# The last piece of the down weights as twelve loads of 11 or 10 rows, and six filler products in place of ten

## The chip, the cores and the metric

The kernel runs on one core of one Trainium2 chip. The metric is the device time of one execution, in microseconds. The kernel before takes 1277.06 us (median of 3 runs, 1276.95 to 1277.29).

## The reference

One decode step of a transformer layer for 4 sequences, all in bf16. First attention over a cache: 32 heads of 128, 8192 cached positions, so that K and V are 256 MB each. Then a gated feed-forward block of width 1792.

```python
x = A_x                                             # 4 x 1 x 512
q = layernorm(x) @ wq                               # 4 x 32 heads x 128
p = softmax(q @ k_cache^T * 128**-0.5)              # 8192 positions
h = x + (p @ v_cache) @ wo
g, u = layernorm(h) @ w_gate, layernorm(h) @ w_up   # 4 x 1792
h2 = h + (sigmoid(g) * u) @ w_down                  # the output
```

## The kernel before, in words

Each engine has a list of instructions of its own, written out in the order in which it is to run them; semaphores join the lists. A helper `emit` appends an instruction with its waits, and `dma` appends a load and hands back a token, a semaphore with the count that it has when the load has landed. A load of the usual kind adds 16 to it.

All inputs but x are loaded by SyncE (SP), on one DMA queue, in the order of the list at the end of the function: wq (L532), then 32 units of K and 32 of V, each unit 4 heads, 8 MB, 128 rows of 64 KB, one for each partition (L541). They go to three slots of SBUF, and a load waits until its slot has been read. DVE transposes a K unit in 16 chunks (L335), TensorE makes the scores of each chunk (L344), the maximum and the exponentials follow (L361 to L369), and TensorE multiplies with V (L405) and adds the unit's result to a bank of PSUM (L415). After the last V unit SP has 40 nops (L543 and L544). Then it waits until the last K unit has been read (`k_done`) and issues wo (L546), the gate weights (L548) and the up weights (L552). Then it waits for `v_done`, a unit of V, and issues the down weights in three pieces (L555 to L558): tiles 0 to 7, 8 to 11, and 12 and 13, by the bounds in `WDT` (L149). Each piece is one load of 128 rows, of 8, 4 and 2 KB a row, with a semaphore of its own.

The tail works on 4 rows. The attention's result is masked and gathered (L454, L461, L466), multiplied with wo (L475) and added to x (L479, L480). A layernorm follows (L273 to L287), the products with gate and up weights (L492, run once for each), sigmoid (L503), and the product of both on DVE in two halves, each transposed (L509, L512). The down product (L521) has 14 tiles with two matmuls each, one for each half of the columns; a tile waits for its half of the transposes and for its piece of the down weights. It adds to the residual, which TensorE has put in the bank before (L516). At the end DVE and ScalarE copy half of the columns each (L529, L530), ScalarE issues the store (L559), and SP waits for its landing.

`filler(n, turns)` (L386 to L388) puts a loop of products on TensorE whose results nobody reads: `n` products of 512 columns in a turn. It stands at three places: 12 turns of 2 ahead of the last product with V (L452), 5 turns of 2 ahead of the product with wo (L467), 5 turns of 2 ahead of the layernorm's transposes (L481).

```python
WDT = (0, 8, 12, 14)                                                            # L149
filler(2, 5)                                                                    # L467
for i in range(len(WDT) - 1):                                                   # L556
    prog.dma("sp", f"wd{i}", lambda e, i=i: e.dma_start(
        wd_v[:, WDT[i]:WDT[i + 1], :], wd_src[:, WDT[i]:WDT[i + 1], :]), [v_done], tok=t_wd[i])
```

Of the kernel before, what the change touches and what calls it, by code (L numbers as in the profile page):

```python
# [18 lines left out]
class _Prog:  # L19
# [52 lines left out]
    def emit(self, eng, fn, waits=(), incs=1, ch=None):  # L72
        todo = self._waits(eng, waits)
        key = ch or eng
        tok = self.token(key, incs) if incs else None
        self._put(eng, todo, key, fn, incs, 1)
        return tok
# [41 lines left out]
def bass_sequential_preLN__mha_block_cached__glu_gated_glu__decode_kernel(  # L119
# [13 lines left out]
    _, H, S, DH = A_k_cache.shape  # L133
# [15 lines left out]
    WDT = (0, 8, 12, 14)  # L149
# [4 lines left out]
    prog = _Prog({"p2d": "dve", "d2d": "dve", "a2d": "dve", "d2p": "pe", "a2p": "pe",  # L154
                  "d2a": "act", "p2a": "act",
                  "k0": "dve", "k1": "dve", "v2": "pe"})
    emit = prog.emit

    with ExitStack() as es:
# [40 lines left out]
        def reg(slot, off, size):  # L200
            return KV[:, slot * SLOT + off:slot * SLOT + off + size]
# [6 lines left out]
        wd_v = reg(2, 0, NFT * D).rearrange("p (t f) -> p t f", t=NFT)  # L208
# [20 lines left out]
        t_wo = prog.token("wo", 16)  # L229
        t_wg = prog.token("wg", 16)  # L230
        t_wu = [prog.token(f"wu{i}", 16) for i in range(len(WUC) - 1)]
        t_wd = [prog.token(f"wd{i}", 16) for i in range(len(WDT) - 1)]

        t_eps = emit("pool", lambda e: e.memset(eps[:, :], EPS))
        t_x = prog.dma("act", "x", lambda e: e.dma_start(x_bf, A_x.rearrange("b s d -> (b s) d")))
# [36 lines left out]
        def layernorm(src, waits, dst):  # L272
            a = emit("dve", lambda e: e.bn_stats(bst, src), waits)  # L273
            a = emit("dve", lambda e: e.bn_aggr(agg, bst), [a])
            a = emit("act", lambda e: e.activation(std[:, 0:1], agg[:, 1:2], ACT.Sqrt, bias=eps[0:B, :]), [a, t_eps])
            a = emit("dve", lambda e: e.reciprocal(std[:, 1:2], std[:, 0:1]), [a])
            t_row = emit("dve", lambda e: e.tensor_scalar(
                row, src, agg[:, 0:1], std[:, 1:2], op0=ALU.subtract, op1=ALU.mult), [a])

            def f(e):  # L280
                ins = None
                for c in range(NC):
                    ins = e.matmul(cols(bank[XS], c), row[:, c:c + NC * 127 + 1:NC], ident[0:B, 0:B],
                                   start=(c == 0), stop=(c == NC - 1), skip_group_check=True)
                return ins
            a = emit("pe", f, [t_row, t_ident])
            return t_row, emit("dve", lambda e: e.tensor_copy(dst, bank[XS][:, 0:NC * B]), [a])  # L287
# [4 lines left out]
        _, t_xn = layernorm(x_bf, [t_x], xnT)  # L292
# [89 lines left out]
        def filler(n, turns=1):  # L382
            if turns > 1:
                prog.open("pe")
            for _ in range(turns):
                if turns > 1:  # L386
                    prog.begin("pe")
                emit("pe", lambda e: [e.matmul(bank[XS], Lq[:, 0:128], Lq[:, 0:512], start=True, stop=True) for _ in range(n)][-1],  # L388
                     [t_ps0, t_lq[NU - 1]], incs=0)
                if turns > 1:  # L390
                    prog.end("pe")
            if turns > 1:
                prog.close("pe")
# [70 lines left out]
            return ins  # L464
        t_rt = emit("pe", f, [t_oa])
        t_ot = emit("dve", lambda e: e.tensor_copy(OT, bank[QB[0]][:, 0:B * WOJ]), [t_rt])  # L466
        filler(2, 5)  # L467

        emit("act", lambda e: e.activation(dummy[:, 0:1], mask[:, 0:1], ACT.Sqrt), [t_mask])

# [54 lines left out]
        for t in range(NFT):  # L525
            if t == 0:
# [6 lines left out]
                 tok=t_wq)  # L533
        for n, (x, u) in enumerate(order):
            w = t_qp if n == 2 else None
            if n >= 3:
# [3 lines left out]
            src = cache[u // (NU // B), HU * (u % (NU // B)):HU * (u % (NU // B) + 1), :, :].rearrange("h (p r) d -> (h p) (r d)", p=32)  # L540
            prog.dma("sp", f"{x}{slot}", lambda e, src=src, slot=slot: e.dma_start(reg(slot, 0, SLOT), src), [w],  # L541
                     tok=toks[x, u])
        for _ in range(40):  # L543
            emit("sp", lambda e: e.nop(), ch="pad")  # L544
        k_done, v_done = t_kd[NU - 1], t_vd[NU - 2]
        prog.dma("sp", "wo", lambda e: e.dma_start(  # L546
# [7 lines left out]
                     [k_done], tok=t_wu[i])  # L554
        wd_src = B_w_down.rearrange("(p t) f -> p t f", p=128)  # L555
        for i in range(len(WDT) - 1):  # L556
            prog.dma("sp", f"wd{i}", lambda e, i=i: e.dma_start(  # L557
                wd_v[:, WDT[i]:WDT[i + 1], :], wd_src[:, WDT[i]:WDT[i + 1], :]), [v_done], tok=t_wd[i])  # L558
        t_out = prog.dma("act", "out0", lambda e: e.dma_start(out.rearrange("b s d -> (b s) d"), o_sb), t_o)  # L559
        emit("sp", lambda e: e.nop(), [t_out], incs=0)  # L560

# [30 lines left out]
```

## Time and profile before

| what | value |
|---|---|
| median of 3 runs | 1277.06 us |
| the profiled execution's own time | 1276.83 us |
| its span, first to last instruction | 1275.6 us |
| mean granted TensorE clock | 0.815 |
| bytes read from HBM | 550.77 MB |
| mean DMA rate over the span | 432 GB/s |

The profile is of one execution, taken by the hardware profiler. Busy times are per engine: PE is TensorE's matmuls, PEld its weight loads, DVE VectorE, ACT ScalarE, SP SyncE. L521 is line 521 of the kernel; all lines of the code from L232 on shift with the edit, L467 to L468 and L557 to L560, for example. In the timeline a row has the start and the length in microseconds, engine, line, operation, what it writes and reads, and in brackets how long the engine was idle ahead of it and what ended that. In the rows of windows there stand, for each stretch, its length, the busy time of PE, PEld, DVE, ACT and POOL with their instruction counts, the granted clock of TensorE, the mean busy share of the 16 DMA engines, and GB/s. A packet is one row of a load or one completion.

### The profile page before, as it was taken

How to read it: one execution, taken by the hardware profiler on the slowest of the kernel's cores; microseconds unless marked ns; L12 is line 12 of the kernel's file. 1: busy time of each engine (PE TensorE's matmuls, PEld its weight loads, DVE VectorE, ACT ScalarE, POOL GpSimd, SP SyncE). 2: the span in 40 equal slices, each digit the busy share in tenths (PEclk: the TensorE clock that was granted, in tenths of full speed). 3: DMA queues.
4: the chain of work that ended last, by engine and by line, in shares of the span. 5: the costliest groups of instructions: out<-in, count | busy, mean ns of one | idle time of the engine just before them, and what ended most of it. 6: DMA issues, size and time to landing. Idle time of an engine off the chain costs nothing.

```text
span 1275.6 us, 14073 instructions
## 1 busy us (share of the span) xinstructions
PE 779.7 (61%) x4588; PEld 328.5 (26%) x4636; DVE 762.3 (60%) x917; ACT 59.0 (5%) x114; POOL 5.7 (0%) x22
## 2 busy tenths in 40 slices
PE   1676755557755557655567655567555577555577
PEld 0232222223222223222222222222222232222233
DVE  1876665556665557665567655566655566655571
ACT  2000000000000000000000000000000000000001
POOL 1000000000000000000000000000000000000000
PEclk8888877788877788877788777788777888777888
DMA  9999999999999999999999999999999999999998
GB/s 423 432 426 430 427 450 434 430 430 427 454 430 430 430 427 454 432 427 430 430 452 432 427 430 434 450 430 427 430 440 444 430 427 430 442 442 430 430 427 371
DMA packets 10244, 550.83 MB, mean 432 GB/s; under 512 B 1144, under 2 KB 1152, under 8 KB 1408
## 3 DMA queue, kind: packets, MB, share of 16 engines
q1 hardware_dynamic: 10224, 550.77, 99.7%
q8 instruction: 2, 0.03, 0.0%
q10 hardware_dynamic: 16, 0.01, 0.0%
q14 instruction: 2, 0.02, 0.0%
HBM read 550.77 MB, written 0.00 MB: 432 GB/s over the span
## 4 chain that ended last, share of the span: by engine, by line
DMA 60%; PE 20%; DVE 12%; issue 2%; ACT 1%; SPq 0%; DVEq 0%
DMA KV<-in_A_k_cache_dram 58%; PE PS L344 14%; DVE kT L335 12%; PE PS L405 5%; DMA KV<-in_B_w_down_dram 3%; ACT kT L410 1%; PE PS L415 0%; SPq L541 0%; DVE PTz L375 0%; PE PS L521 0%; DVE KV L529 0%; SPq L557 0%; DVEq L112 0%
## 5 line engine op out<-in xcount | busy, mean ns | idle before, releaser
L344 PE MATMUL PS<-kT,Lq 128*128 128x512 bf16 x2048 | 588.7, 420 | 343.5 <-DVE kT L335 326.4
L335 DVE STREAM_TRANSPOSE kT<-KV 128x1024 f32<-128x1024 f32 x512 | 614.4, 1232 | 300.3 <-DMA KV<-in_A_k_cache_dram 237.5
L344 PEld LDWEIGHTS PS<-kT,Lq 128*128 x2048 | 210.3, 103 | 694.6 <-issue 621.7
L375 DVE STREAM_TRANSPOSE PTz<-E_sb 32x512 bf16<-32x512 bf16 x128 | 89.9, 703 | 129.1 <-PE PS L415 125.5
L405 PE MATMUL PS<-KV,PTz 128*16 128x512 bf16 x2048 | 117.0, 381 | 0.0
L379 PE MATMUL PS<-part,headw 128*128 128x2 f32 x64 | 18.8, 363 | 100.4 <-DVE PTz L375 100.4
L369 ACT ACTIVATE E_sb<-PS,negm 128x512 bf16<-128x512 f32 x32 | 22.0, 687 | 1139.4 <-DVE negm L367 1139.4
L405 PEld LDWEIGHTS PS<-KV,PTz 128*16 128x16 bf16 x2048 | 58.9, 111 | 56.3 <-issue 13.6
L415 PE MATMUL PS<-lane,kT 128*128 128x4 f32 x256 | 33.6, 255 | 31.0 <-ACT kT L410 31.0
L362 DVE TENSOR_REDUCE part<-PS 128x1 f32<-128x512 f32 x32 | 22.1, 691 | 38.7 <-PE PS L344 38.7
L415 PEld LDWEIGHTS PS<-lane,kT 128*128 128x128 f32 x256 | 31.0, 191 | 46.2 <-issue 44.8
L379 PEld LDWEIGHTS PS<-part,headw 128*128 128x128 f32 x64 | 16.0, 310 | 103.7 <-DVE PTz L375 103.7
L410 ACT ACTIVATE kT<-PS,rsb 128x512 f32<-128x512 f32 x32 | 22.0, 687 | 61.5 <-PE PS L405 61.5
L388 PE MATMUL PS<-Lq 128*128 128x512 bf16 x27 | 11.0, 462 | 2.9 <-issue 2.5
L328 DVE TENSOR_TENSOR Lq<-q_all,mask 128x32 bf16<-128x32 bf16 x32 | 9.5, 297 | 0.0
L454 DVE TENSOR_TENSOR kT<-PS,mask 128x512 bf16<-128x512 f32 x1 | 0.7, 692 | 13.3 <-PE PS L415 13.3
L367 DVE STREAM_TRANSPOSE negm<-mxr 128x32 f32<-128x32 f32 x32 | 6.8, 212 | 1.1
L364 DVE STREAM_TRANSPOSE turn<-part 128x32 f32<-128x32 f32 x32 | 6.8, 211 | 1.1
L388 PEld LDWEIGHTS PS<-Lq 128*128 128x128 bf16 x44 | 4.8, 116 | 8.3 <-issue 6.1
L322 PEld LDWEIGHTS PS<-Lq,headw 128*128 128x128 bf16 x32 | 3.5, 108 | 12.8 <-issue 11.3
L396 DVE RECIPROCAL rsb<-PS 128x1 f32<-128x1 f32 x32 | 6.3, 197 | 0.7 <-PE PS L379 0.7
L301 PE MATMUL PS<-KV,kT 128*4 128x512 bf16 x32 | 3.6, 627 | 5.0 <-DMA KV<-in_A_wq_dram 5.0
(70 smaller groups left out, 56.7 us busy)
## 6 DMA issues: line engine op xcount, KB each, us to landing
KV<-in_A_wq_dram SPq DMA_DIRECT2D x1, 4096.0 KB, 12.2
KV<-in_A_wo_dram SPq DMA_DIRECT2D x1, 4096.0 KB, 27.2
KV<-in_B_w_gate_dram SPq DMA_DIRECT2D x1, 1792.0 KB, 31.1
KV<-in_B_w_up_dram SPq DMA_DIRECT2D x1, 1792.0 KB, 34.9
KV<-in_B_w_down_dram SPq DMA_DIRECT2D x1, 1024.0 KB, 32.1
KV<-in_A_k_cache_dram SPq DMA_DIRECT2D x32, 49.6
KV<-in_A_v_cache_dram SPq DMA_DIRECT2D x32, 30.7
KV<-in_B_w_down_dram SPq DMA_DIRECT2D x1, 512.0 KB, 32.9
```

The source lines that it names most:

```text
L328: t_lq[u] = emit("dve", lambda e, ix: e.tensor_tensor(dst, bass.AP(raw(q_all), at(ix, 0) * (4 * TU) + 4 * (u - TU * t), [[NU * 4, 128], [1 ...
L335: t_tr[u, c] = emit("dve", lambda e: e.transpose(kT[:, (c % 2) * TW:(c % 2 + 1) * TW], KVw[:, o:o + TW]), w, ch="d2p")
L344: ins = e.matmul(bank[SBK], bass.AP(raw(Lq), ix[-1] * 2 + (128 * t + c % 2), [[528, 128], [1, 128]]), rhs, start=False, stop=False, skip_g ...
L362: a = emit("dve", lambda e: e.tensor_reduce(part[:, 0:1], bank[SBK], AX.X, ALU.max), [t_sc[u, NT - 1], t_pool], ch="d2d")
L364: a = emit("dve", lambda e: e.transpose(turn_[:, :], part[:, :]), [a], ch="d2d")
L369: t_exp[u] = emit("act", lambda e: e.activation(E_sb[:, :], bank[SBK], ACT.Exp, bias=negm[:, 0:1], scale=SCALE, accum_out=part[:, 1:2]), [ ...
L375: return [e.transpose(PTz[32 * q:32 * (q + 1), :].rearrange("p (r q c) -> p r q c", r=4, q=4)[:, :, q, :], E_sb[32 * q:32 * (q + 1), :].re ...
L379: t_sum[u] = emit("pe", lambda e: e.matmul(bank[QB[1]][:, 0:2], headw[:, :], part[:, 0:2], start=True, stop=True), [t_ptz[u], t_selc], ch= ...
L388: emit("pe", lambda e: [e.matmul(bank[XS], Lq[:, 0:128], Lq[:, 0:512], start=True, stop=True) for _ in range(n)][-1], [t_ps0, t_lq[NU - 1] ...
L405: made.append(e.matmul(PS[32 * j:32 * j + 16, ob:ob + 512], lhsT, KV[:, slot * SLOT + 512 * k:slot * SLOT + 512 * (k + 1)], start=(k < 4), ...
L410: t_ocp[u] = emit("act", lambda e: e.activation(O_sb, bank[OBK], ACT.Copy, scale=rsb[:, 0:1]), [t_pv[u], t_rs[u]], ch="a2p")
L415: ins = e.matmul(bass.AP(raw(PS), at(ix, 0) * 4 + (512 * EX + 4 * (u - t)), [[4096, 128], [1, 4]]), O_sb[:, 128 * q:128 * (q + 1)], lane[: ...
```

## The change

The third piece of the down weights, tiles 12 and 13, is no longer one load of 128 rows of 2 KB. It is twelve loads: load `a`, for `a` from 0 to 11, has the rows and partitions a, a + 12, a + 24 and so on, 11 rows for `a` under 8 and 10 rows for the others. All twelve add to the same semaphore, on whose count of 192 the last two tiles wait. The first two pieces are as before. Since SP issues 11 DMAs more, the nops ahead of wo are 29 in place of 40. The filler ahead of the product with wo has 3 turns in place of 5, so six products in place of ten.

```diff
-        t_wd = [prog.token(f"wd{i}", 16) for i in range(len(WDT) - 1)]
+        LAST = [(a, 11 if a < 8 else 10) for a in range(12)]
+        t_wd = [prog.token(f"wd{i}", 16 * (len(LAST) if i == len(WDT) - 2 else 1)) for i in range(len(WDT) - 1)]
...
-        filler(2, 5)
+        filler(2, 3)
...
-        for _ in range(40):
+        for _ in range(29):
             emit("sp", lambda e: e.nop(), ch="pad")
...
-            prog.dma("sp", f"wd{i}", lambda e, i=i: e.dma_start(
-                wd_v[:, WDT[i]:WDT[i + 1], :], wd_src[:, WDT[i]:WDT[i + 1], :]), [v_done], tok=t_wd[i])
+            for a, n in (LAST if i == len(WDT) - 2 else ((0, 0),)):
+                rows = slice(a, a + 12 * (n - 1) + 1, 12) if n else slice(0, 128)
+                prog.dma("sp", f"wd{i}", lambda e, i=i, rows=rows: e.dma_start(
+                    wd_v[rows, WDT[i]:WDT[i + 1], :], wd_src[rows, WDT[i]:WDT[i + 1], :]), [v_done], tok=t_wd[i])
```

## Prediction

> **What bounds the kernel now.** I read the page first (busy shares, the slices, the chain that ended last), then the end of the run: the DMA share in windows, the timeline of the last microseconds, the DMA issues with their times to landing.
>
> ```profile
> PE 779.7 (61%) x4588; PEld 328.5 (26%) x4636; DVE 762.3 (60%) x917; ACT 59.0 (5%) x114; POOL 5.7 (0%) x22
> DMA  9999999999999999999999999999999999999998
> DMA packets 10244, 550.83 MB, mean 432 GB/s; under 512 B 1144, under 2 KB 1152, under 8 KB 1408
> q1 hardware_dynamic: 10224, 550.77, 99.7%
> q10 hardware_dynamic: 16, 0.01, 0.0%
> DMA 60%; PE 20%; DVE 12%; issue 2%; ACT 1%; SPq 0%; DVEq 0%
> ```
>
> No compute engine is over 61% busy, while the sixteen DMA engines (I call each a lane) are busy in every slice. 432 GB/s over 16 lanes is 27 GB/s a lane. Nothing in the change alters the 550 MB, so only the last few microseconds can move. The end of the run in windows (the last two columns are the mean busy share of the 16 lanes, and GB/s):
>
> ```profile
> 1270.50:1271.30 0.80, 0.46 (x4) 0.00 (x0) 0.64 (x2) 0.00 (x0) 0.00 (x0) 1.00 0.97 387
> 1271.30:1271.70 0.40, 0.07 (x2) 0.10 (x4) 0.40 (x2) 0.00 (x0) 0.00 (x0) 1.00 0.56 215
> 1271.70:1273.00 1.30, 1.22 (x22) 0.77 (x23) 0.45 (x2) 0.00 (x0) 0.00 (x0) 1.00 0.16 61
> 1273.00:1273.80 0.80, 0.74 (x12) 0.15 (x6) 0.00 (x0) 0.00 (x0) 0.00 (x0) 1.00 0.00 0
> ```
>
> The share falls from 0.97 to 0.16, which is 2.6 of 16 lanes, and stays there for 1.3 us: most lanes are done by about 1271.5, and two or three run about 1.3 us behind. They don't speed up when the others stop (61 GB/s over 2.6 lanes is 23), so a lane has a limit of its own. The kernel's end hangs on the late lanes:
>
> ```profile
> 1239.43 1.28 SPq L557 DMA_DIRECT2D KV<-in_B_w_down_dram  x3
> 1271.60 0.78 PEld L521 LDWEIGHTS PS<-KV 128*4 128x4 bf16 x16 [1.15 <-DVE KV L512]
> 1272.75 0.31 PEld L521 LDWEIGHTS PS<-KV 128*4 128x4 bf16 x8 [0.37 <-DMA KV<-in_B_w_down_dram]
> 1273.39 0.09 PEld L521 LDWEIGHTS PS<-KV 128*4 128x4 bf16 x4 [0.33 <-DMA KV<-in_B_w_down_dram]
> 1273.85 0.38 ACT L530 ACTIVATE KV<-PS 4x256 bf16<-4x256 f32 x1 [3.50 <-PE PS L521]
> 1274.31 0.27 ACTq L559 DMA_DIRECT2D out_dram<-KV  x1
> KV<-in_B_w_down_dram SPq DMA_DIRECT2D x1, 1024.0 KB, 32.1
> KV<-in_B_w_down_dram SPq DMA_DIRECT2D x1, 512.0 KB, 32.9
> KV<-in_B_w_down_dram SPq DMA_DIRECT2D x1, 256.0 KB, 33.1
> ```
>
> The reader is to see two waits in a row. The four tiles of the middle piece start at 1272.75 after 0.37 us of idling for their DMA, the two of the last piece at 1273.39 after 0.33 us more. Copies follow at 1273.85, the store at 1274.31, the end at 1275.6. The span of 1275.6 belongs to an execution of 1276.83 us (1.23 outside it); the median shown, 1277.06, is 0.23 above that execution. I sum against 1276.83 and add 0.23.
>
> **The change part by part.** *The fillers.* Rows around L467, in which L388 is the filler and L475 the product with wo:
>
> ```profile
> 1259.55 0.63 PE L388 MATMUL PS<-Lq 128*128 128x512 bf16 x1 [0.22 <-issue]
> 1260.41 0.63 PE L388 MATMUL PS<-Lq 128*128 128x512 bf16 x1 [0.22 <-issue]
> 1261.82 2.22 PE L475 MATMUL PS<-KV,kT 128*4 128x512 bf16 x32
> 1268.74 1.69 PE L492 MATMUL PS<-KV,kT 128*4 128x448 bf16 x32 [0.27 <-DVE kT L287]
> 1271.05 0.41 DVE L512 STREAM_TRANSPOSE KV<-KV 128x224 bf16<-128x224 bf16 x1
> 1271.77 0.41 DVE L512 STREAM_TRANSPOSE KV<-KV 128x224 bf16<-128x224 bf16 x1
> 1233.33 0.33 SPq L546 DMA_DIRECT2D KV<-in_A_wo_dram  x1
> KV<-in_A_wo_dram SPq DMA_DIRECT2D x1, 4096.0 KB, 27.2
> 1234.18 0.42 SPq L552 DMA_DIRECT2D KV<-in_B_w_up_dram  x1
> KV<-in_B_w_up_dram SPq DMA_DIRECT2D x1, 1792.0 KB, 34.9
> 1245.40:1248.80 3.40, 2.51 (x5) 1.18 (x8) 0.00 (x0) 0.00 (x0) 0.00 (x0) 0.50 0.78 337
> 1259.10:1262.50 3.40, 2.74 (x12) 1.03 (x18) 0.00 (x0) 0.00 (x0) 0.00 (x0) 0.50 0.97 417
> 1262.50:1265.90 3.40, 2.61 (x31) 0.66 (x24) 0.01 (x1) 0.60 (x1) 0.00 (x0) 1.00 0.99 422
> ```
>
> A turn of two fillers takes 0.86 us at the granted clock of 0.50 (1260.41 less 1259.55); two of five turns go, 1.7 us. wo lands at 1233.33 + 27.2 = 1260.5, so L475 starts at about 1260.6 in place of 1261.82. Until 1262.5 the clock is 0.50: of the 1.2 us won, half is lost again to products run at half clock, so L475 ends 0.6 us earlier, and the layernorm and L492 come 0.6 us earlier (1268.1). The first 16 products of L492 need half of 1.69, to 1268.95; the other 16 need the up weights, which land at 1234.18 + 34.9 = 1269.1. They start at 1269.1 in place of 1269.5: 0.4 us of the 0.6 is left. So the transposes of L512 end at 1271.06 and 1271.78, in place of 1271.46 and 1272.18. There it stops: the first L521 product waits for the first down piece (1239.43 + 32.1 = 1271.5), and the middle piece is later still. **Zero at the end.** If the cover by the DMAs were gone, it would be worth 0.4 us. The clock could undo it: the window 1259.10:1262.50 has 2.74 us of PE work now and about 2.8 to 2.9 after (1.0 of fillers, 1.9 of L475); one with 2.51 at the same clock was followed by full clock. I take no change of clock; another 3.4 us at half clock would delay L475 by up to 0.9 us and the chain after it by at most that much again, most of it in the slack that the down pieces leave: 0 to +0.5.
>
> *SP.* Eleven nops go and eleven DMAs come. Three issues took 1.28 us at L557, so 0.43 each; fourteen end at 1239.43 + 6.0 = 1245.4, 26 us ahead of need, and nothing of SP's is behind them but the last wait. The nops lie before the wait for k_done at L546 (28.6 us of waiting below). Zero.
>
> ```profile
> SPq L546 <- DVE dumm L361: 28.6, 1, 28.6
> GB/s 0 0 0 0 0 0 0 0 0 0 0 0 0 0 0 0 0 0 0 0 0 20 41 21 0 0 0 0 0 0 0 0 0 0 0 0 0 0 0 0
> q10 hardware_dynamic: 8, 0.00, 0.7%
> ```
>
> *The loads.* How many lanes does a load of 11 rows use? The 71 loads of 128 rows on q1 have 9088 rows; 10224 packets less these is 1136 = 71 x 16 completions. The store of four rows (last two rows above, the window 1274 to 1276 in 40 slices of 0.05 us) left 8 packets: four rows, four completions. So a DMA of four rows goes to four lanes with one row and one completion each, and I take 11 and 10 lanes for 11 and 10 rows. In all: ten lanes get 12 rows and 12 completions, one gets 8 and 8, five get none, where each had 8 and one. Packets on q1: 10224 + 128 - 16 = 10336.
>
> From the middle to the last piece the late lanes need 1273.39 - 1272.75 = 0.64 us for 8 rows and a completion; 16 KB at 27 GB/s is 0.60, so a completion costs at most 0.04. Twelve rows and completions cost 0.96 to 1.4 us. The punctual lanes, done at about 1271.5, start the last piece 0.64 before that, at 1270.9, and so end by 1271.9 to 1272.3. If the late lanes are among the five, the last piece no longer ends last.
>
> Next late is then the **middle piece**, which stays on all sixteen lanes and lands for PE at 1272.75 + x, where x is what the new loads do to the late lanes. Four more weight loads, two pairs of products, take 0.31 - 0.09 = 0.22 us, 0.11 a pair. The middle piece's four pairs take 0.44; from the first product of the last piece to the copies it is 1273.85 - 1273.39 = 0.46. The copies start at 1272.75 + x + 0.44 + 0.46 = 1273.65 + x, against 1273.85: **the end moves by x - 0.20.**
>
> x lies between 0 and 0.64. Zero, if a lane's 27 GB/s is a limit of the sender, since the late senders have no more to do than before up to the middle piece. [...] I take the upper end, because the other way in which the late lanes can hurt (below) comes out near it: +0.44.
>
> [...]
>
> **The rivals.**
>
> *Forecast, 0.42:* the writes collide, x is near 0.64. 1276.83 + 0.44 + 0.23 = 1277.50; its own range is 1277.1 to 1277.7, x from 0.24 to 0.84.
>
> *A, the late lanes are relieved, 0.26:* they are among the five, and x is 0. -0.20: 1276.86. For it: the drain at 0.16 is just the work that is taken off them. Against: the last piece is only 0.64 us of a lag of 1.3, and PE is busy 0.44 of those 0.64 anyway.
>
> *B, a late lane is among the eleven, 0.22:* it takes the last piece from 1272.75 on with 12 rows in place of 8: 1273.71 to 1274.15, later by 0.32 to 0.76. 1277.38 to 1277.82. For it: eleven of sixteen lanes are used, and no view says which lanes are late. Against: only 1272.75 stands for all late lanes; one of them may be less late. [...]
>
> *C, slower by more than the bound, 0.05:* a completion holds its lane until its rows are confirmed. Place: the eleven lanes, between rows. The price per completion p makes the last piece 12 x (0.08 + p) long from 1270.9 on; it passes the old landing of 1273.39 from p = 0.13 on and costs over 2.55 us (0.2%) from p = 0.34 on. The store is the nearest row for a whole confirmation: from its packets (1275.05 to 1275.2, slices 22 to 24 above) to the end at 1275.6, p is about 0.4, and the piece would land at 1276.7: +3.3, 1280.4. Against: at most 0.04 between the middle and the last piece, as worked out above.
>
> *D, the loads don't spread, 0.03:* 128 rows on one lane are 128 x 0.08 = 10 us from 1270.9: 1280.9, +7.5, 1284.6. Against: the store's eight packets.
>
> **How the numbers follow.** The forecast with A and B holds 0.90; C, D and the unforeseen 0.10. Predicted: 1277.50. The range goes from A with 0.26 for the scatter of runs and a smaller gain, 1276.6, to the upper end of B with as much, 1278.1. A measurement of this kernel tells about 0.2% (2.55 us) from no change, and the forecast, A and B all lie within that. Slower by over 0.2%: C and D, 0.08. Faster by over 0.2%: 0.01, the half of the unforeseen (no case here is worth 2.5 us). Same: 0.90 and the other 0.01, 0.91.
>
> **What would show it.** Fillers: L475 starts at about 1260.6, the first L521 load still at 1271.6. Loads: 10336 packets on q1, twelve issues at L560 of 0.43 us each. Forecast: the wait before the middle piece's products ends later than 1272.75, at up to 1273.39, and there is no wait before the last four. A: it ends at 1272.75 with no wait behind it, copies at 1273.65. B: the middle piece at 1272.75 and the last four products at 1273.7 or later. C and D: a wait of microseconds before the last four products. Wrong altogether would be a time outside 1276.6 to 1278.1, above all from a change before 1258, where nothing was edited.

## The result, and the profile after

The changed kernel takes 1278.69 us (median of 22 runs, 1277.93 to 1279.42), the kernel before 1276.95 in the same comparison (22 runs, 1276.61 to 1277.39). The ratio is 1.0014, with a 95% interval of 1.0008 to 1.0020: slower by 1.7 us, small but real. The predicted time was 1277.50, with a range up to 1278.1. The profiled execution after took 1278.33 us, 1.50 more than the one before.

The page after, in the rows that answer to those shown of before:

```profile
PE 779.2 (61%) x4586; PEld 327.8 (26%) x4632; DVE 762.4 (60%) x917; ACT 58.9 (5%) x114; POOL 5.7 (0%) x22
DMA  9999999999999999999999999999999999999998
DMA packets 10356, 550.83 MB, mean 431 GB/s; under 512 B 1256, under 2 KB 1264, under 8 KB 1520
q1 hardware_dynamic: 10336, 550.77, 99.6%
```

Bytes and busy times are the old ones, and the packets on q1 are the 10336 that the prediction worked out. The second half of the up products starts at 1269.02, where the prediction had 1269.1 for the landing of their weights in before. So all of it lies in the microseconds behind that. The timeline of after, from the product with wo on:

```profile
1260.54 1.93 PE L476 MATMUL PS<-KV,kT 128*4 128x512 bf16 x32 [0.55 <-DMA KV<-in_A_wo_dram]
1269.02 0.93 PE L493 MATMUL PS<-KV,kT 128*4 128x448 bf16 x16 [0.91 <-DMA KV<-in_B_w_up_dram]
1271.71 0.78 PEld L522 LDWEIGHTS PS<-KV 128*4 128x4 bf16 x16 [1.75 <-DVE KV L513]
1273.42 0.31 PEld L522 LDWEIGHTS PS<-KV 128*4 128x4 bf16 x8 [0.93 <-DMA KV<-in_B_w_down_dram]
1273.42 0.60 PE L522 MATMUL PS<-KV 128*4 128x256 bf16 x8 [0.63 <-DMA KV<-in_B_w_down_dram]
1274.87 0.09 PEld L522 LDWEIGHTS PS<-KV 128*4 128x4 bf16 x4 [1.15 <-DMA KV<-in_B_w_down_dram]
1274.88 0.38 PE L522 MATMUL PS<-KV 128*4 128x256 bf16 x4 [0.86 <-DMA KV<-in_B_w_down_dram]
1275.33 0.37 ACT L531 ACTIVATE KV<-PS 4x256 bf16<-4x256 f32 x1 [6.55 <-PE PS L522]
```

And TensorE's own rows of the down product in before, which the prediction did not show, from the timeline and from the view by line:

```profile
1271.63 2.15 PE L521 MATMUL PS<-KV 128*4 128x256 bf16 x28 [0.68 <-DMA KV<-in_B_w_down_dram]
L521 PE MATMUL PS<-KV x28: 269/272/273, 1271.6 to 1273.5; 128*4 128x256 bf16 x28
```

The reader is to see that before, all 28 products stand in one row of 2.15 us, and that this row hides two waits: each product counts for 0.27 us, while a pair starts 0.11 us behind the last, so a short wait doesn't break the row. The weight loads' rows in the prediction show the waits. The trace also records when each lane's completion reaches its semaphore; I call that a landing. In before the last of the sixteen landings is at 1272.71 for the middle piece and at 1273.35 for the last, and the weight loads follow 0.04 us behind each. After, these landings are at 1273.37 and 1274.83. The waits are longer and break the row in three, with 0.63 us of idling for the middle piece and 0.86 us for the last. From start to start, the middle piece's products come 0.67 later (1273.42 less 1272.75). The last piece could then be used at 1273.42 + 0.44 = 1273.86, and its products start at 1274.87, 1.01 later still. The copies move from 1273.85 to 1275.33, 1.48 of the 1.50 us.

The windows of after, with the DMA share and GB/s in the last two columns:

```profile
1270.50:1271.30 0.80, 0.00 (x0) 0.00 (x0) 0.73 (x4) 0.00 (x0) 0.00 (x0) 1.00 0.94 356
1271.30:1271.70 0.40, 0.00 (x0) 0.00 (x0) 0.40 (x1) 0.00 (x0) 0.00 (x0) 1.00 0.88 262
1271.70:1273.00 1.30, 1.04 (x16) 0.66 (x16) 0.00 (x0) 0.00 (x0) 0.00 (x0) 1.00 0.23 66
1273.00:1273.80 0.80, 0.38 (x8) 0.27 (x8) 0.00 (x0) 0.00 (x0) 0.00 (x0) 1.00 0.02 5
```

From 1271.3 to 1271.7 the lanes are busy for 0.88 (0.56 before) and move 262 GB/s: 0.88 x 16 lanes are 14, so 19 GB/s each, where before had 24 in the same stretch (215 over 0.56 x 16). And after 1273.2 there is no packet at all until the store, as the DMA view of after from 1273.2 to 1276 has it:

```profile
DMA packets 0, 0.00 MB, mean 0 GB/s; under 512 B 0, under 2 KB 0, under 8 KB 0
```

The last packet began at least 1.67 us before the products that wait for it (1274.87 less 1273.2). That time carries no data, only landings: four of the last five, which I take for one lane's, are 0.18 us apart, at 1274.29, 1274.47, 1274.65 and 1274.83 (the fifth is at 1274.34). The packet records show the lane that sent last: its rows start 0.086 us apart, and all twelve rows and completions go out from 1272.14 to 1273.18.

### The profile page after: what moved, and what is told of

It reads as the page before. It is cut to its first block, busy times and chain, and to the rows that moved or that the text cites. A ratio compares the mean times of both kernels' runs of the same rounds, so it can differ in the third digit from the quotient of the medians.

```text
span 1277.1 us, 14063 instructions
## 1 busy us (share of the span) xinstructions
PE 779.2 (61%) x4586; PEld 327.8 (26%) x4632; DVE 762.4 (60%) x917; ACT 58.9 (5%) x114; POOL 5.7 (0%) x22
## 3 DMA queue, kind: packets, MB, share of 16 engines
q1 hardware_dynamic: 10336, 550.77, 99.6%
## 4 chain that ended last, share of the span: by engine, by line
DMA 60%; PE 19%; DVE 13%; issue 2%; SPq 1%; ACT 1%; DVEq 0%
DMA KV<-in_A_k_cache_dram 58%; PE PS L345 14%; DVE kT L336 13%; PE PS L406 5%; DMA KV<-in_B_w_down_dram 2%; ACT kT L411 1%; SPq L560 1%; PE PS L416 0%; SPq L542 0%; DVE PTz L376 0%; PE PS L522 0%; DVE KV L530 0%; DVEq L112 0%
## 5 line engine op out<-in xcount | busy, mean ns | idle before, releaser
L366 DVE TENSOR_SCALAR_CACHE_REDUCE turn<-turn 128x32 f32<-128x32 f32 x32 | 6.0, 187 | 1.1
```

## The experiments

Two terms were to be told apart. For the last piece: it is late because each of its twelve loads costs a lane a time of its own, whatever its size (as in rival C), or because a late lane now has twelve rows in place of eight (rival B). For the middle piece: it is late because rows sent by other lanes go to the partitions that a late lane is still filling (the forecast), or because the new loads get in its way somewhere else. Where a letter stands in an expectation without more, the text below it says what it stood for. The diffs are shortened; in every run the number of nops ahead of wo makes up for the loads added or taken away.

**Each edit alone.** First the fillers:

```diff
-        filler(2, 5)
+        filler(2, 3)
```

> The kernel before with only the filler loop cut from five turns to three. Both theories of the loss (theory L: the loss is all in how the last piece is loaded; rival F: a part of it comes from the fillers, through the clock or the order of the tail) are told apart here. L: within 0.1 us of the kernel before (1276.95), the product with wo starts about 1.2 us earlier, the down products of the first piece at the same time. F: slower by 0.5 us or more.

1276.82 us (11 runs, 1276.56 to 1277.18) against 1276.93; ratio 0.9999, 0.9990 to 1.0008. The timeline:

```profile
1260.62 1.90 PE L475 MATMUL PS<-KV,kT 128*4 128x512 bf16 x32
1271.46 0.77 PEld L521 LDWEIGHTS PS<-KV 128*4 128x4 bf16 x16 [1.55 <-DVE KV L509]
1272.63 0.31 PEld L521 LDWEIGHTS PS<-KV 128*4 128x4 bf16 x8 [0.39 <-DMA KV<-in_B_w_down_dram]
1273.27 0.09 PEld L521 LDWEIGHTS PS<-KV 128*4 128x4 bf16 x4 [0.33 <-DMA KV<-in_B_w_down_dram]
```

The product with wo starts 1.2 us earlier, and the end moves by 0.1: the fillers are worth nothing, as forecast. Then the loads, with the fillers as before:

```diff
-        filler(2, 3)
+        filler(2, 5)
```

> The changed kernel with the five turns of fillers put back, so only the twelve loads (and the 29 nops) are new. L: the whole loss, 1278.4 to 1279.0, with the same two waits before the middle and the last down products. F: clearly nearer to the kernel before, under 1278.0.

1278.93 us (11 runs, 1277.97 to 1279.64); ratio 1.0015, 1.0006 to 1.0025. All of the loss is the loads'. In its timeline the middle piece's products start at 1273.65 and the last piece's at 1274.58, so both waits are there, shared out otherwise than in after.

**Probes behind the old last piece.** Before, with five small loads at the end of the queue and a memset on POOL as a mark behind each; they are extra work.

```diff
+        for n in (4, 8, 11, 13, 16):
+            t_p = dma(reg(2, 16384 + 256 * n, 256)[0:n, :], wd_src[0:n, 0, 0:256])
+            emit("pool", memset(spare[:, n:n + 1]), [t_p])
```

> The kernel before with five small loads of 4, 8, 11, 13 and 16 rows of 512 B behind the last piece, each waited for by GpSimd with a memset, so the memsets tell when the first 4, 8, 11, 13, 16 lanes are through. Theory B (a late lane is among the eleven that the twelve loads use): the memset for 11 comes about 1 us or more after the punctual lanes' time (about 1272.3), at 1273 or later. Rival (all late lanes are among the other five, and the loss of the last piece is all in its completions): the memset for 11 at about 1272.5, and the jump of 0.7 us or more only at 13 or 16.

The five marks in one row of the timeline of e3:

```profile
1273.18 0.82 POOL L563 MEMSET spare<- 128x1 f32 x5 [1265.73 <-DMA KV<-in_B_w_down_dram]
```

The jump came where neither theory had put it, at the first load. Four rows suffice to be late: three of the four landings come at 1272.19 to 1272.38, the fourth at 1273.14, and the mark at 1273.18. So one of the first four lanes is late, and the eleven cannot all be punctual. The two latest lanes, which land the old last piece at 1273.35 and 1273.47 in this run, are others: two landings that late first appear with the load of 13 rows (1273.52 and 1273.62). If the nth row goes to the nth lane, they are the 12th and 13th, outside the eleven. The other four marks follow (0.82 - 0.10) / 4 = 0.18 us apart, for rows of 512 bytes that need 0.02 us at 27 GB/s. That spacing was the first hint at what a load costs by itself.

**Eight rows on every lane.** The last piece of after as eight loads of 16 rows: each of the sixteen lanes has its eight rows, as before, but eight completions in place of one.

```diff
-        LAST = [(a, 11 if a < 8 else 10) for a in range(12)]
+        LAST = [(a, 16) for a in range(8)]
-                rows = slice(a, a + 12 * (n - 1) + 1, 12) if n else slice(0, 128)
+                rows = slice(a, a + 8 * (n - 1) + 1, 8) if n else slice(0, 128)
```

> The changed kernel with the last piece as eight loads of 16 rows, 8 partitions apart: all sixteen lanes, 8 rows a lane as in the kernel before, but eight completions in place of one. Theory C in a small form: the late lanes' last piece takes 8 x 0.18 = 1.4 us in place of 0.64, so the last products start 0.8 us later or more: 1277.7 to 1278.3. Rival B (the loss of the last piece is that a late lane gets 12 rows in place of 8): 1276.9 to 1277.3.

1278.49 us (11 runs, 1278.20 to 1278.95) against 1276.79; ratio 1.0014, 1.0005 to 1.0023. Its timeline:

```profile
1273.59 0.43 PEld L522 LDWEIGHTS PS<-KV 128*4 128x4 bf16 x8 [0.75 <-DMA KV<-in_B_w_down_dram]
1275.04 0.09 PEld L522 LDWEIGHTS PS<-KV 128*4 128x4 bf16 x4 [1.01 <-DMA KV<-in_B_w_down_dram]
```

No lane has more rows than before, and yet 1.45 us lie between the middle and the last piece, where 0.64 did. That is 8 x 0.18. Rival B alone is refuted. The time lies above both expected ranges: C's left out the middle piece's delay, which is here too (1273.59 against 1272.75), and the granted clock was 0.50 in the last products, so that the copies start 0.66 us behind their first (1275.70), not 0.46.

**Two loads.** The other way: 121 and 7 rows, two completions a lane at most.

```diff
+        LAST = [(0, 121), (121, 7)]
+                rows = slice(a, a + n) if n else slice(0, 128)
```

> [...] Theory C in a small form: most of the wait before the last products goes, 10 x 0.1 to 0.16 us, and 1277.2 to 1277.6 is left, by the delay x of the middle piece alone (+0.44 in the prediction's sum). If x were the only loss: no change against the changed kernel, 1278.7. If sending were the limit and not the partitions: 1276.7, faster than the kernel before.

1277.97 us (11 runs, 1277.39 to 1278.40); ratio 1.0009, 0.9999 to 1.0018, so slower or the same. The timeline of its profiled execution, 1277.48 us:

```profile
1260.87 3.58 PE L476 MATMUL PS<-KV,kT 128*4 128x512 bf16 x32 [0.75 <-DMA KV<-in_A_wo_dram]
1272.42 0.78 PEld L522 LDWEIGHTS PS<-KV 128*4 128x4 bf16 x16 [1.56 <-DVE KV L510]
1272.45 1.98 PE L522 MATMUL PS<-KV 128*4 128x256 bf16 x28 [1.09 <-DMA KV<-in_B_w_down_dram]
1273.61 0.53 PEld L522 LDWEIGHTS PS<-KV 128*4 128x4 bf16 x12 [0.41 <-DMA KV<-in_B_w_down_dram]
```

The twelve weight loads of the middle and the last piece stand in one row: with two completions a lane at most the last piece causes no wait. They wait for the middle piece (last landing 1273.56) and start at 1273.61, 0.86 later than in before. So this run shows the forecast's sum by itself: x - 0.20 is 0.66 with x = 0.86, and the profiled executions are 0.65 apart. The first piece was late too, with its last landing at 1272.32 against 1271.50, but its 16 weight loads are through by 1273.20 and so don't set the end. The median is 1.18 us above before's 1276.79 and above the expected 1277.2 to 1277.6; no trace shows what the slower executions add.

**What a load of one row a lane costs.** Before, with marked blocks of loads behind the last piece; they are extra work. First twelve loads in a block, 11 rows each:

```diff
+        # behind wd, each block with a token of its own and a POOL mark:
+        # one load of 24 KB rows; 12 of 2 KB; 12 of 512 B; 12 of 2 KB on neighbouring partitions
```

> The kernel before with five blocks of loads of 11 rows behind the last piece, on scratch rows, each block waited for by GpSimd with a memset: one load of 2 KB rows (the start mark); one load of 24 KB rows; twelve of 2 KB rows, 12 partitions apart; twelve of 512 B rows, 12 apart; twelve of 2 KB rows on eleven neighbouring partitions. Theory C in a small form (a completion holds its lane until its row is confirmed; the run with small loads behind the last piece had 0.18 us from one to the next): 0.9, 2.2, 2.1 us, so the same for 2 KB and for 512 B. Rival (a completion costs at most 0.04, as the prediction had it): 0.9, 0.9 to 1.4, 0.3 to 0.7 us. [...]

The marks of e5:

```profile
1273.67 0.10 POOL L567 MEMSET spare<- 128x1 f32 x1 [1266.22 <-DMA KV<-in_A_wo_dram]
1274.54 0.10 POOL L567 MEMSET spare<- 128x1 f32 x1 [0.77 <-DMA KV<-in_A_wo_dram]
1277.05 0.10 POOL L567 MEMSET spare<- 128x1 f32 x1 [2.40 <-DMA KV<-in_A_wo_dram]
1279.91 0.10 POOL L567 MEMSET spare<- 128x1 f32 x1 [2.76 <-DMA KV<-in_A_wo_dram]
1282.17 0.10 POOL L567 MEMSET spare<- 128x1 f32 x1 [2.17 <-DMA KV<-in_A_wo_dram]
```

One load of 24 KB a lane takes 0.87 us (1274.54 less 1273.67). The same bytes in twelve loads take 2.51, a quarter of the bytes in twelve loads 2.86. Bytes don't set it; the number of loads does. Both blocks of twelve took longer than C's 2.2 and 2.1. The last block, on neighbouring partitions, is not longer (2.26); but a mark follows the latest lane alone, and others can be far ahead of it (the sixteen landings of before's middle piece lie between 1270.98 and 1272.71), so this says little about the partitions. Then with four and eight rows a load, four partitions apart:

```diff
+        block(0, 8, 0, 24576, 256, 1)     # i, rows (by fours), first partition, column, elements, loads
+        block(1, 4, 0, 16384, 256, 12)
+        block(2, 8, 0, 20480, 256, 12)
+        block(3, 8, 32, 20480, 1024, 12)
```

> The kernel before with four blocks of loads behind the last piece, on scratch rows that by the trace of the last two runs are the lanes' own (by fours from 0 or 32), each block waited for by GpSimd: one load of 8 rows of 512 B (the mark); twelve loads of 4 rows of 512 B; twelve of 8 rows of 512 B; twelve of 8 rows of 2 KB. Theory C (each completion holds its own lane, about 0.2 us, whatever the others do): 2.0 to 2.9 us for each block of twelve. Rival G (completions of all lanes go through one place, one in 0.019 us, which gave the 2.51 and 2.86 us for 132 of them): 0.9, 1.8, 1.8 us. Rival N (rows on other lanes' partitions made the loads slow, not the completions): 0.3, 0.4 and 1.0 us. The middle and the last down products start as in the kernel before, 1272.75 and 1273.39, give or take 0.1.

```profile
1272.91 0.10 POOL L567 MEMSET spare<- 128x1 f32 x1 [1265.45 <-DMA KV<-in_A_wo_dram]
1275.12 0.10 POOL L567 MEMSET spare<- 128x1 f32 x1 [2.12 <-DMA KV<-in_A_wo_dram]
1277.52 0.10 POOL L567 MEMSET spare<- 128x1 f32 x1 [2.29 <-DMA KV<-in_A_wo_dram]
1279.93 0.10 POOL L567 MEMSET spare<- 128x1 f32 x1 [2.32 <-DMA KV<-in_A_wo_dram]
```

2.21 us for twelve loads of four rows of 512 bytes, 2.40 for eight rows, 2.41 for eight rows of 2 KB: **0.18 to 0.20 us from one landing to the next on a lane**, for 512 bytes and 2 KB and for four and eight lanes. C holds as a time per completion, but not as a lane that stands still meanwhile: in after the rows went out 0.086 us apart, and only the landings fell behind. G (0.9, 1.8 and 1.8 for the three blocks) and N (0.3, 0.4 and 1.0) fall. The last landing in after comes 1.66 us behind the last packet (1274.83 less 1273.17); what takes the 0.18 us, no run shows.

**The middle piece: which partitions.** After, with the twelve loads' rows sent to a scratch area on partitions 0 to 50:

```diff
-                    wd_v[rows, WDT[i]:WDT[i + 1], :], ...
+                    reg(2, 16384 + 1024 * a, 1024)[0:5 * n - 4:5, :], ...
```

> The changed kernel, but the rows of the twelve loads are written to scratch columns of partitions 0 to 50 (the two last tiles of the down weights are not loaded, and old values of the buffer stand there). So the lanes send the same, and no row goes to partitions 64 to 127, where the lanes that are latest (among lanes 11 and 12, by the run with small loads) would write theirs, if each lane has a fixed group of partitions. Theory P (the delay x of the middle piece comes from rows written to the partitions of the late lanes): the middle products start at 1272.6 to 1272.8 again. Rival S (x is something that the many small loads do to all lanes): 1273.4 again. The last products, by theory C in a small form, start at 1273.9 or later in either case.

1279.00 us (10 runs, 1278.71 to 1279.89); ratio 1.0018, 1.0009 to 1.0028. The middle piece's products start at 1273.32, so the delay stayed, and theory P as it was put, that only the late lanes' partitions matter and that they lie elsewhere, failed. One reading, argued and not shown: one of the late lanes is among the first four (e3), and all 256 KB now go to partitions 0 to 50. What slowed the late lanes in e6 stays open. The next pair was made so that only the order of partitions differs; `own` and `foreign` are theory O's names for them, and no run shows which lane writes which partitions. Before, with six loads of eight rows of 16 KB at the end of the queue (extra work):

```diff
+        # own = partitions 0, 4 .. 28 and 32 .. 60; shift = 4 .. 32; foreign = 64 .. 92 and 96 .. 124
+        # e9:  own, own, shift, foreign, foreign, 40 .. 47
+        # e10: foreign, foreign, shift, own, own, 40 .. 47
```

> The kernel before with six loads of 8 rows of 16 KB behind the last piece, on scratch rows and lanes 0 to 7, each waited for by GpSimd: partitions 0, 4 .. 28; 32, 36 .. 60; 4, 8 .. 32; 64, 68 .. 92; 96, 100 .. 124; 40 to 47. [...] Theory O (rows on partitions that are not the lane's own slow it and the late lanes; x is that): the first two blocks take 0.60 to 0.65 us, the third to fifth clearly more, and the middle down products start at 1272.75 as in the kernel before, since the late lanes are through when the foreign rows begin. Rival T (any rows that other lanes send beside the late lanes slow these): the middle products start at 1273.0 or later. [...]

> The same six loads, the two of partitions 64 to 92 and 96 to 124 first. Theory O: the middle down products start 0.3 us or more later than in the other order, since lanes 0 to 7 now write the late lanes' partitions while these are still at work. Rival T: as in the other order.

The timelines of e9 and of e10, the last two groups of weight loads:

```profile
1272.78 0.31 PEld L522 LDWEIGHTS PS<-KV 128*4 128x4 bf16 x8 [0.38 <-DMA KV<-in_B_w_down_dram]
1273.43 0.09 PEld L522 LDWEIGHTS PS<-KV 128*4 128x4 bf16 x4 [0.35 <-DMA KV<-in_B_w_down_dram]
```

```profile
1272.22 1.04 PE L522 MATMUL PS<-KV 128*4 128x256 bf16 x16 [0.56 <-DVE KV L513]
1273.74 0.31 PEld L522 LDWEIGHTS PS<-KV 128*4 128x4 bf16 x8 [0.72 <-DMA KV<-in_B_w_down_dram]
1274.89 0.09 PEld L522 LDWEIGHTS PS<-KV 128*4 128x4 bf16 x4 [0.84 <-DMA KV<-in_B_w_down_dram]
```

With the blocks called own first, both pieces come as in before (1272.78 and 1273.43, against 1272.75 and 1273.39). With partitions 64 to 124 first, the middle piece comes 0.96 later and the last 1.46. The tail of e10 was late too, but not the cause: its first sixteen products ended at 1272.22 + 1.04 = 1273.26, and TensorE waited from there. Bytes, loads, rows and completions are the same in both; **in this pair, one run each, the order of the partitions decides**. The reading is that the punctual lanes run ahead into the extra rows, which stand behind both pieces in the queue, and slow the lanes that still fill those partitions.

The packet records agree. In e9 every 16 KB row that starts before 1273.0 takes 0.611 us, as O expected; in e10 those from 1272.1 on are held up, to as much as 1.19 us. O's "clearly more" for the third to fifth block of e9 failed: most of those rows take 0.611 us too, and the marks (1.08, 0.39, 1.32, 0.66 and 0.60 us apart) follow the latest lane alone. So it is not a foreign partition as such that costs.

Two more runs bear on rival S, that many small loads delay the middle piece as such. The 37 loads of e12, on partitions 0 to 60 by fours, did not delay it (last landing 1272.80, and its products run on behind the first piece's in one row). In e5, whose first loads have rows 12 partitions apart, the second with 24 KB a row, it came late:

```profile
1271.94 1.94 PE L522 MATMUL PS<-KV 128*4 128x256 bf16 x28 [0.56 <-DVE KV L513]
```

```profile
1273.51 0.31 PEld L522 LDWEIGHTS PS<-KV 128*4 128x4 bf16 x8 [0.95 <-DMA KV<-in_B_w_down_dram]
```

Over all the runs, the middle piece's own rows tell the two cases apart. Each of its 128 packets of 4 KB takes 0.159 us in before, e1, e3, e9 and e12, and its last landing there is between 1272.59 and 1272.85. In after, e2, e5, e6, e7, e8, e10 and e11, 2 to 15 of them take over 0.17 us, the longest 0.21 to 0.39 us, and the last landing is between 1273.28 and 1273.70.

So the partitions matter by 0.96 us in e10 against e9; a rate per group of partitions was not measured.

**The reading side.** After, with the twelve loads reading old K rows in SBUF, not HBM:

```diff
-                    wd_src[rows, WDT[i]:WDT[i + 1], :]
+                    reg(1, 30720, 1024)[rows, :]
```

> The changed kernel with the twelve loads reading from SBUF (old K rows of the same partitions) in place of HBM: the two last tiles of the down weights hold old K values, everything else is the same, the completions too. Theory H (x comes from the reading side, small rows of HBM read by eleven lanes): the middle products start at 1272.75 again. Rival (it comes from the writing side): 1273.3 or later again. The wait before the last products, by the completions, stays in both: 1274.5 or later.

1278.26 us in one run. The timeline of e11:

```profile
1273.54 0.52 PEld L522 LDWEIGHTS PS<-KV 128*4 128x4 bf16 x8 [0.83 <-DMA KV<-in_B_w_down_dram]
1274.60 0.09 PEld L522 LDWEIGHTS PS<-KV 128*4 128x4 bf16 x4 [0.55 <-DMA KV<-KV]
```

Both delays are there without the reads from HBM. It is not the reading of the new loads that delays the middle piece.

## Why the prediction was wrong

*Right: where to look.* Only the last microseconds moved, and the down weights' landing sets them.

*Right: the fillers.* The product with wo starts at 1260.54 (about 1260.6 foretold), and e1 puts the time at 1276.82 against 1276.93. The clock went the better way: the product took 1.90 us in e1 and 1.93 in after, in place of the half-clock time that was assumed. That is luck of these executions: with the same three turns it took 2.63 to 3.58 us in e6, e7, e8 and e11. In e1 the gain is worth nothing because the transposes were ready at 1270.93 and the first piece landed at 1271.36.

*Right in result, wrong in size: SP.* The view by line of after's issues:

```profile
L560 SPq DMA_DIRECT2D KV<-in_B_w_down_dram x14: 328/745/908, 1239.0 to 1248.6; - x14
```

A load of 11 or 10 rows takes SP 0.745 us to issue (median), not 0.43. It is not the number of rows: of the loads of 11 neighbouring rows in e5, nine issues take 3.46 us, 0.38 each. The last issue starts at 1248.6, still over 20 us ahead of need: zero.

*Right: the loads spread.* 10336 packets on q1. D fell.

*Right: the middle piece.* x was taken as 0.64, and 1273.42 less 1272.75 is 0.67; it would have moved the end by 0.47, as e7 shows by itself. That the size fits so well is partly luck: 0.64 was the upper end of the prediction's range for x, and in the changed kernel and its variants (e2, e6, e7, e8, e11) the last landing of the middle piece is 0.57 to 0.90 later than in before. No run shows the 0.64 as a limit of the partitions written; what the runs showed in its place are these delays, and 0.96 in e10 against e9. That pair speaks for the cause that was forecast, e11 excludes the new loads' reads, and e6 doesn't fit the simple form. A fell with its x at zero, though its condition held for the two latest lanes (e3, if the nth row goes to the nth lane).

*Wrong, the failing step:* **"a completion costs at most 0.04"**, and with it "twelve rows and completions cost 0.96 to 1.4 us" and "the last piece no longer ends last". The 0.64 us between the middle and the last piece was a true gap between landings (1272.71 and 1273.35). But in that gap one completion stands behind 0.60 us of data, so it bounds what a completion takes to send, and says nothing of how fast completions land when only one row lies between them. Sending was priced rightly: the completion's packet takes 0.009 us, and the lane that sent last needed 1.04 us for its twelve rows and completions. The landings are the step that was left out: on one lane they come 0.18 to 0.20 us apart (e12; e3 and e5 have 0.18 to 0.24), so twelve of them take 2.2 to 2.4 us (e12), not 0.96 to 1.4.

*Wrong with it: that the eleven lanes may be taken as punctual.* In before, the landings of the middle piece are at 1271.44 or earlier on twelve lanes, at 1271.60 and 1271.90 on the next two, and at 1272.59 and 1272.71 on the latest two. By e3, if the nth row goes to the nth lane, the latest two are not among the eleven, but a late lane is; I take it for the third-latest. In after that lane's share of the middle piece lands at 1272.61, 0.71 later than in before, and 12 x 0.185 behind that is 1274.83, the last landing of the last piece. The same sum holds in e2, e6 and e11, within 0.05 us. A punctual lane at the same price, from 1271.46 on, would be through by 1273.7, before the 1273.86 at which the last piece could be used. So the wait of 1.01 us is **B's place with C's price**, on a lane that the collision had made later still: rivals that had been weighed one at a time came together. C's price itself, in the prediction's form 12 x (0.08 + p), is p = 0.10 to 0.12, below the 0.13 from which it was to matter on a punctual lane, and far from the 0.4 read off the store. And e8 shows that the price costs as much without B's extra rows.

*The sum.* x - 0.20 with x = 0.67 gives +0.47, the term that was missing +1.01; together 1.48 of the 1.50 us. In e7, with two completions a lane at most, the first term stands alone.

*Open.* Why three lanes are late; why the landings of a lane are 0.18 us apart; why e6 kept the middle piece's delay; and why the runs after scatter over 1.5 us where those before stay within 0.8.

## What to carry to other kernels

Cut a late load into as few DMAs as will do: with one row a lane, each DMA's completion landed 0.18 to 0.20 us behind the one before it on its lane, more than twice the 0.08 us of a 2 KB row, and whatever waits for the last of them waits for all (1.01 us in after). Moving rows off a late lane did not relieve it here; what the runs showed is that the order of the partitions written by loads behind a piece in the queue moved that piece by 0.96 us (e10 against e9); that rows to the partitions which a lane is still filling slow it is the reading of this. A price read from one gap holds for the pattern of that gap: a completion behind 0.60 us of data does not tell what a completion behind 0.08 us costs. And a row of many short instructions can hide a wait; look at what feeds it, here the weight loads.

## What the runs showed of the hardware

- Completions of loads with one row a lane land 0.18 to 0.20 us apart on their lane, for 512 bytes and 2 KB and for four and eight lanes (e12), while the rows can go out 0.086 us apart (after).
- The last packet can lie far ahead of what waits for its landing: at least 1.67 us in after, with no packet on any queue from 1273.2 to 1276.
- With six loads of eight rows of 16 KB behind it in the queue, a piece landed for TensorE 0.96 us later when those to partitions 64 to 124 came first than when those to 0 to 60 did (e10 against e9, one run each).
- A 4 KB row of a piece takes 0.159 us undisturbed, and up to 0.39 us in the runs whose middle piece lands late (e2).
- Issuing a load of 11 or 10 rows that lie 12 partitions apart takes SP 0.745 us, against 0.43 for one of 128 rows and 0.38 for 11 neighbouring rows (e5, nine issues in 3.46).
